# Background matmul groups of an attention and FFN kernel: where in a slot they stand and which of them share one

## The chip, the cores and the metric

The kernel runs on 1 core of a Trainium2 chip. The metric is the device time of one execution in microseconds.

## The reference

For each of 8 batches and 8 heads, `a` is the softmax of `phi` (576 x 32) over its 32 memories. From it come `k_m = a^T k` and `v_m = a^T v` (32 x 64). The scores are `q k_m^T / 8`, again with a softmax over the 32 memories, and multiplied by `v_m`. The heads are put side by side into `x` (4608 x 512), and the output is `silu(x w_in) w_out` with 2048 hidden columns. All inputs are float32.

```python
a = phi - np.max(phi, axis=2, keepdims=True)
a = np.exp(a)
a = a / (np.sum(a, axis=2, keepdims=True) + 1e-09)
k_m = np.einsum('bhsm,bhsd->bhmd', a, k)
v_m = np.einsum('bhsm,bhsd->bhmd', a, v)
```

A constant subtracted from all of `phi` in one softmax row cancels, so any shift that keeps exp in range gives the same result.

## The kernel before

**Slots.** The work goes batch by batch. A batch has 16 slots, one for each chunk `fc` of 128 hidden columns. In a slot TensorE does FFN1 of that chunk (`ffn1`, L583, twelve matmuls of 288 columns into the two banks of the tile `h`), then FFN2 of the chunk before (`main_step`, L639, with `ffn2`, L627: four tiles of 128 tokens, three matmuls of 512 columns each, into four accumulator banks). ScalarE applies silu to `h` (`silu`, L610, two activations: 512 columns into `g`, 64 leftover columns into `gleft`), and VectorE splits `g` into a high and a low float32r part (`split`, L599: a cast on L605, a subtract on L607). `h` has a single buffer, so FFN1 of the next slot waits until everything that touches `h` is done. After every second batch come four steps with the leftover tokens (`left_step`).

**Background.** While batch b runs, the attention of batch n = b + 1 is prepared by small steps, each tied to a slot (L658 to L697; `fc + 0.5` is the second half of a slot). In the order of the work they are:

- `phi_max` and `phi_fold` (VectorE): maxima of phi over the rows, folded over the partitions, so that each head and half has one value to subtract; the batch b = 0 uses `phi_allmax` with two small matmuls for it
- `phi_sub` (VectorE, L291 and L295) and `phi_exp` (ScalarE, L299)
- `e_mm`, here "e": `k_m`, `v_m` and the sums of `a`, 64 matmuls (L311) and 16 (L319) of 129 columns in array tiles of 128x32 and 64x32; its readers on VectorE and ScalarE (L327 to L335) write the normalised `kvn`
- `e_tr`, "the turn": two 128x128 transposes of `kvn` into `kvT`
- `s_mm`, the scores of one half of the tokens: 16 matmuls of 288 columns in 64x32 array tiles, then `s_turn`, two VectorE transposes back (L369)
- `s_max`, `s_sub`, `s_exp`, `s_sum`, `s_norm`, `s_back`, `s_low`: the second softmax, its transposes and the high and low part that FFN1 reads
- `p_mm`, "P": `w_in` multiplied by `v_m`, 16 matmuls of 512 columns in 64x32 array tiles for a quarter of the hidden columns (256 columns in batch 0), which ScalarE copies (L577) and VectorE subtracts (L579) into a high and a low part; FFN1 then multiplies these parts by the attention weights. A batch's own P of j = 1 to 3 stand in its slots 1, 5 and 9, and the P of j = 0 of the next batch in slot 14.

One call of a matmul on plain float32 shows as two instructions in the profile. e, the turn (from n = 2 on), the scores and P all write to one pair of banks, the tile `bg`, which also has a single buffer.

**Order.** The main loop (L803 to L823) issues FFN1, silu and split of a slot, then the first two FFN2 tiles, the steps of slot `fc`, the last two FFN2 tiles, and the steps of slot `fc + 0.5`. On TensorE and SP a written order holds up to batch 1; VectorE and ScalarE are ordered by hand only in the first stage. For the rest the framework orders the instructions of an engine by when it expects their inputs. It also puts waits between any two engines that touch one PSUM bank of a tile.

**DMA.** Loads of phi, kv, q and the stores are issued on SP. kv and q wait for the buffers that e and the scores free, phi for the one that the scores' turn back frees.

```python
            h = ffn1(b, fc)
            gs = split(silu(b, fc, h))
            for part in range(2):
                finish((2 * part, 2 * part + 1))
                for fn, a in events.pop((b, fc + part / 2), []):
                    fn(*a)
            prev = ("main", b, fc, gs)
```

Of the kernel before, what the change touches and what calls it, by code (L numbers as in the profile page):

```python
# [10 lines left out]
F32 = mybir.dt.float32  # L11
# [5 lines left out]
ALU = mybir.AluOpType  # L17
AX = mybir.AxisListType

P = 128  # L20
# [28 lines left out]
def attn_ffn_kernel(  # L49
# [149 lines left out]
    def banks(b):  # L199
# [2 lines left out]
        bg = bgtile()  # L202
        return [bg[:, 0], bg[:, 1]]

    def load_phi(b):
        t = sb.tile([P, PHW], F32, tag="att", name=f"phi{b}")
        at[b]["e"] = t[:, : FULLC * HM].rearrange("p (g c f) -> p g c f", g=2, c=FULLC)
        at[b]["er"] = t[:, FULLC * HM :]
        at[b]["et"] = t
        w = FULLC * P  # L210
        for f in ((0, w), (2 * w, PHW), (w, 2 * w)) if b == 0 else ((0, PHW),):
            load(t[:, f[0] : f[1]], phi[b, :, f[0] : f[1]])
# [17 lines left out]
    def rows(p):  # L230
        return slice(REST * p, REST * (p + 1))
# [13 lines left out]
    def phi_allmax(b, ps_=(0, 1), steps=(0, 1)):  # L245
        n = len(ps_)
        if 0 in steps:
            bank = banks(b)[0] if b else ps.tile([P, 512], F32, tag="acc", name="firstm", bufs=NI)
            pt = bank[:, : n * P]
            cm = sb.tile([P, 2], F32, tag="cm", name="cm", bufs=2)  # L250
            for i, p in enumerate(ps_):
                nc.tensor.transpose(pt[:, i * P : (i + 1) * P], at[b]["mx"][:, p], ident)
            nc.vector.tensor_reduce(cm[:, :n], pt.rearrange("p (g f) -> p g f", g=n), op=ALU.max, axis=AX.X)
            at[b]["cm"] = cm, bank[:, HM : HM + n * P]
        if 1 in steps:
            cm, pm = at[b]["cm"]
            for i in range(n):
                nc.tensor.matmul(
                    pm[:, i * P : (i + 1) * P], cm[:, i : i + 1].broadcast_to([P, P]), ident,
                    start=True, stop=True, skip_group_check=True,  # L260
                )
            at[b]["am"] = pm.rearrange("p (g f) -> p g f", g=n)

    def phi_fold(b, step):
        if step == 0:
            t = sb.tile([P, HM], F32, tag="am", name="mxt", bufs=1)
            nc.vector.transpose(t, at[b]["mx"].rearrange("p g f -> p (g f)"))
            qm = sb.tile([P, H], F32, tag="qm", name="qm", bufs=1)
            nc.vector.tensor_reduce(qm, t.rearrange("p (n m) -> p n m", m=M), op=ALU.max, axis=AX.X)
            at[b]["qm"] = qm  # L270
        elif step == 1:
            qm = at[b]["qm"]
            z = sb.tile([M, 4, H], F32, tag="qz", name="qz", bufs=1)
            for i in range(4):
                nc.vector.tensor_copy(z[:, i], qm[M * i : M * (i + 1)])  # L275
            fm = sb.tile([P, H], F32, tag="fm", name="fm", bufs=1)
            nc.vector.tensor_reduce(fm[:M], z.rearrange("p i n -> p n i"), op=ALU.max, axis=AX.X)
            for i in range(1, 4):
                nc.vector.tensor_copy(fm[M * i : M * (i + 1)], fm[:M])
            at[b]["fm"] = fm  # L280
        else:
            am = sb.tile([P, HM], F32, tag="am", name="am", bufs=1)
            wide = sb.tile([P, H, M], F32, tag="mx", name="wide", bufs=1)
            nc.vector.tensor_copy(wide, at[b]["fm"].unsqueeze(2).broadcast_to([P, H, M]))
            nc.vector.transpose(am, wide.rearrange("p n m -> p (n m)"))
            at[b]["am"] = am.rearrange("p (g f) -> p g f", g=2)

    def phi_sub(b, ps_=(0, 1)):
        e, er, am = at[b]["e"], at[b]["er"], at[b]["am"]
        g = slice(ps_[0], ps_[-1] + 1)  # L290
        nc.vector.tensor_tensor(  # L291
            e[:, g], e[:, g], am.unsqueeze(2).broadcast_to([P, len(ps_), FULLC, P]), op=ALU.subtract
        )
        for i, p in enumerate(ps_):
            nc.vector.tensor_tensor(er[rows(p)], er[rows(p)], am[rows(p), i], op=ALU.subtract)  # L295

    def phi_exp(b, ps_=(0, 1)):
        if len(ps_) == 2:
# [5 lines left out]

    def e_mm(b):
        e, er, kvt, kr = (at[b][k] for k in ("e", "er", "kv", "kr"))
        pt = banks(b)
        turns = [(c, p) for c in range(FULLC) for p in range(2)]
        for c, p in turns:
            for r in range(NR):  # L310
# [24 lines left out]
                nc.vector.tensor_scalar(kvn[:, :, p], src, rs[p], None, op0=ALU.mult)  # L335

    def e_tr(b):
        if b > 1:
            bg = bgtile()
            pt = [bg[:, 0, P * kind : P * (kind + 1)] for kind in range(2)]  # L340
        else:
            pt = [live["h"][:, kind, HALF : HALF + P] for kind in range(2)]
        t = sb.tile([P, 2, NR, M], F32, tag="kvT", name=f"kvT{b}", bufs=2)
        for kind in range(2):
            nc.tensor.transpose(pt[kind], kvn[:, kind].rearrange("p g d -> p (g d)"), ident)
        nc.vector.tensor_copy(t[:, 0].rearrange("p r m -> p (r m)"), pt[0])
        nc.scalar.copy(t[:, 1].rearrange("p r m -> p (r m)"), pt[1])
        at[b]["kvT"] = t

    def s_mm(b, hf):  # L350
        if "sc" not in at[b]:
# [304 lines left out]
        events.setdefault((b, slot), []).append((fn, a))  # L656

    for b in range(B):  # L658
        if b == 0:
            for j in range(2, DFF // CW):  # L660
                ev(b, 2 * j - 1.5, p_mm, b, j * CW, CW)
        else:
            for j in range(1, NJ):
                ev(b, 4 * j - 3, p_mm, b, j * JW, JW)
        n = b + 1
        if n == B:
            continue
        at_slot = (4, 5, 6, 7.5, 9, 9.5, 11.5, 11.5, 12, 12.5, 12.5, 13) if b == 0 else (0, 1, 2, 3, 4, 6, 7, 8, 9, 10, 11, 12)
        mx, sub, ex, em, tr, s0, s1, sx, se, ss, sn, sk = at_slot
        ev(b, mx, phi_max, n)  # L670
        if n == 1:
# [8 lines left out]
        if n + 1 < B:  # L680
            ev(b, 14 if b == 0 else em + 1, load_kv, n + 1)
        ev(b, tr, e_tr, n)
        ev(b, s0, s_mm, n, 0)
        ev(b, em, load_q, n, 1)
        ev(b, s1, s_mm, n, 1)
        if n + 1 < B:
            ev(b, s1, load_q, n + 1, 0)
        ev(b, sx, s_max, n, ALL)
# [15 lines left out]
        getattr(mybir.EngineType, e) for e in ("PE", "DVE", "Activation", "SP")  # L704
    )
    whole = ExitStack()
    whole.enter_context(in_order(PE, SP))
    load_phi(0)
    I0, O0, I1 = ("i", 0), ("o", 0), next(to_conv)
    idle = ps.tile([P, 2, 512], F32, tag="h", name="idle", bufs=1)[:, 0]  # L710
# [92 lines left out]
    for b in range(B):  # L803
        if b == 1:
            whole.close()
        for fc in range(NFC):
            if b == 0 and fc < 2:
# [3 lines that stand above are left out]
                continue  # L811
            h = ffn1(b, fc)
            gs = split(silu(b, fc, h))
            for part in range(2):
                finish((2 * part, 2 * part + 1))
                for fn, a in events.pop((b, fc + part / 2), []):
                    fn(*a)
            prev = ("main", b, fc, gs)
        if b % 2:
            for n in range(NLS):  # L820
                gs = split(gleft[:, n * NI : (n + 1) * NI].rearrange("p c f -> p (c f)"))
                finish((0, 1, 2, 3))
                prev = ("left", b, n, gs)  # L823
# [56 lines left out]
```

## Time and profile before

| | us |
|---|---|
| median of 3 runs (lowest to highest) | 713.63 (712.69 to 713.66) |
| the profiled execution, its own time | 711.86 |
| its span, first to last instruction | 710.1 |
| TensorE matmuls busy | 696.2 (98%) |
| VectorE busy | 366.3 (52%) |
| ScalarE busy | 258.5 (36%) |

The granted TensorE clock is 0.999 of full speed over the span. The chain of work that ended last lies to 83% on TensorE. The profile names TensorE's matmuls PE, its weight loads PEld, VectorE DVE, ScalarE ACT and SyncE SP. A line of the timeline gives the start and the duration in us, then engine, line, operation, the tiles written and read, the array tile, shape and count; the bracket at its end is the engine's idle time before it and what released it. Matmuls are pipelined: their durations overlap, so what a matmul costs is read from the distance between starts.

### The profile page before, as it was taken

Reading aid. Unit: us, or ns where it says so; the run is one execution under the profiler, and the core shown is the slowest. Engines: PE = TensorE matmul, PEld = TensorE weight load, DVE = VectorE, ACT = ScalarE, POOL = GpSimd, SP = SyncE. Lnnn points to the kernel's source line nnn. Section 1 sums busy time; section 2 is a strip of 40 time slices with the busy share of each in tenths; the row PEclk is TensorE's granted clock in tenths of the full one; section 3 lists DMA queues with packets and bytes.
Section 4 is the critical chain, followed back from the end, with each engine's and each line's share of the span. In section 5 each row is a group of like instructions: output and inputs, shape, how many; then the busy total and the mean of one; then the engine's idle time right before and its main releaser. Section 6 shows DMA issues by size and latency. Waiting matters only on the chain.

```text
span 710.1 us, 11571 instructions
## 1 busy us (share of the span) xinstructions
PE 696.2 (98%) x4833; PEld 556.1 (78%) x4833; DVE 366.3 (52%) x658; ACT 258.5 (36%) x454; POOL 0.7 (0%) x6
## 2 busy tenths in 40 slices
PE   7899999999999999999999999999999999999997
PEld 3577678788888788777887778887888878888885
DVE  3899886355353563538246373535635356233322
ACT  2789854233323332424224241423322323222211
POOL 0000000000000000000000000000000000000000
PEclk9999999999999999999999999999999999999999
DMA  9977615321113210232011420132101000010002
GB/s 341 387 243 235 245 38 224 135 67 35 45 31 135 67 34 1 83 146 68 1 60 20 153 76 3 61 135 67 34 15 60 2 1 1 0 61 1 1 1 74
DMA packets 25444, 60.14 MB, mean 85 GB/s; under 512 B 2096, under 2 KB 10416, under 8 KB 25392
## 3 DMA queue, kind: packets, MB, share of 16 engines
q1 hardware_dynamic: 24672, 57.02, 23.0%
q10 hardware_dynamic: 720, 2.38, 0.9%
q8 instruction: 38, 0.62, 0.4%
q14 instruction: 14, 0.11, 0.1%
HBM read 49.95 MB, written 9.44 MB: 84 GB/s over the span
## 4 chain that ended last, share of the span: by engine, by line
PE 83%; DVE 3%; ACT 2%; DMA 1%; issue 0%; ACTq 0%
PE acc L627 44%; PE h L593 25%; PE accleft L627 6%; PE bg L563 4%; PE bg L311 2%; PE bg L357 1%; DMA raw<-in_w_out 1%; DVE gparts L607 1%; ACT L613 1%; DVE phi L291 1%; ACT phi L299 0%; ACT pparts L577 0%; PE bg L319 0%; DVE qz L275 0%; ACT g L613 0%
## 5 line engine op out<-in xcount | busy, mean ns | idle before, releaser
L627 PE MATMUL acc<-wo_hi,gparts 128*128 128x512 f32 x1024 | 352.5, 397 | 0.3 <-DVE gparts L607 0.3
L627 PEld LDWEIGHTS acc<-wo_hi,gparts 128*128 128x128 f32 x1024 | 191.9, 188 | 66.9 <-issue 29.8
L593 PEld LDWEIGHTS h<-aparts,pparts 128*128 128x128 f32 x1536 | 215.2, 188 | 17.8 <-ACT gleft L615 4.7
L593 PE MATMUL h<-aparts,pparts 128*128 128x288 f32 x1536 | 225.9, 296 | 1.6 <-ACT gleft L615 0.8
L627 PE MATMUL acc<-wo_lo,gparts 128*128 128x512 f32 x512 | 201.2, 393 | 0.4 <-DVE wo_lo L176 0.4
L613 ACT ACTIVATE g<-h 128x512 f32<-128x512 f32 x128 | 76.4, 597 | 303.4 <-issue 175.4
L605 DVE CAST gparts<-g 128x512 fp32r<-128x512 f32 x128 | 54.5, 426 | 222.0 <-ACT g L613 221.2
L627 PEld LDWEIGHTS acc<-wo_lo,gparts 128*128 128x128 f32 x512 | 96.1, 188 | 15.2 <-DVE wo_lo L176 0.7
L607 DVE TENSOR_TENSOR gparts<-g,gparts 128x512 fp32r<-128x512 f32 x128 | 88.2, 689 | 10.5 <-DVE gparts L605 0.5
L579 DVE TENSOR_TENSOR pparts<-bg,pparts 128x1024 fp32r<-128x1024 f32 (+1 forms) x36 | 39.6, 1099 | 36.2 <-ACT pparts L577 36.2
L577 ACT ACTIVATE pparts<-bg 128x1024 fp32r<-128x1024 f32 (+1 forms) x36 | 33.4, 927 | 27.8 <-PE bg L563 27.8
L627 PE MATMUL accleft<-wo_hi,gparts 128*128 128x512 f32 x128 | 40.6, 389 | 0.0
L563 PE MATMUL bg<-win,kvT 64*32 64x512 f32 (+1 forms) x576 | 35.8, 554 | 0.9 <-DVE kvn L335 0.9
L615 ACT ACTIVATE gleft<-h 128x64 f32<-128x64 f32 x128 | 28.0, 218 | 0.0
L627 PEld LDWEIGHTS accleft<-wo_hi,gparts 128*128 128x128 f32 x128 | 24.0, 188 | 4.9
L633 ACT ACTIVATE o<-acc 128x512 f32<-128x512 f32 x32 | 19.2, 599 | 21.9 <-PE acc L627 10.7
L627 PE MATMUL accleft<-wo_lo,gparts 128*128 128x512 f32 x64 | 24.9, 389 | 0.0
L613 ACT ACT_TABLE_LOAD x14 | 18.0, 1283 | 8.0 <-PE h L593 7.9
L563 PEld LDWEIGHTS bg<-win,kvT 64*32 64x32 f32 x576 | 6.5, 104 | 14.1 <-issue 11.7
L605 DVE CAST gparts<-gleft 128x512 fp32r<-128x512 f32 x16 | 6.8, 427 | 20.3 <-PE accleft L627 11.9
L168 ACT ACTIVATE raw<-raw 128x1024 int32<-128x1024 uint32 (+1 forms) x16 | 16.7, 1041 | 0.0
L395 DVE TENSOR_REDUCE ssm<-sc 128x36 f32<-128x1152 f32 x7 | 9.5, 1354 | 8.8 <-ACT sc L391 8.8
(126 smaller groups left out, 365.6 us busy)
## 6 DMA issues: line engine op xcount, KB each, us to landing
kv<-in_kv SPq DMA_DIRECT2D x28, 516.0 KB, 5.7
q<-in_q SPq DMA_DIRECT2D x16, 576.0 KB, 3.8
out<-o SPq DMA_DIRECT2D x32, 256.0 KB, 2.1
raw<-in_w_in SPq DMA_DIRECT2D x14, 512.0 KB, 6.4
raw<-in_w_out SPq DMA_DIRECT2D x6, 1024.0 KB, 7.3
phi<-in_phi SPq DMA_DIRECT2D x7, 576.0 KB, 3.7
kv<-in_kv ACTq DMA_DIRECT2D x4, 516.0 KB, 6.0
kr<-in_kv SPq DMA_DIRECT2D x7, 258.0 KB, 7.2
```

The source lines that it names most:

```text
L168: nc.scalar.activation(r, low, AF.Copy, scale=2.0**-29)
L311: nc.tensor.matmul(pt[p][M * r : M * (r + 1), :KVW], e[:, p, c, M * r : M * (r + 1)], kvt[c][:, p, r], start=c == 0, stop=False, skip_grou ...
L563: nc.tensor.matmul(bg[M * r : M * (r + 1), p, :w].rearrange("p (k f) -> p k f", f=P), kvT[D * p : D * (p + 1), 1, r], win[D * p : D * (p + ...
L577: nc.scalar.activation(hi[:, :, c], bg[:, :, :w], AF.Copy)
L579: nc.vector.tensor_tensor(lo[:, :, c], bg[:, :, :w], hi[:, :, c], op=ALU.subtract)
L593: nc.tensor.matmul(h[:, hf, :HALF], wt[:, p, fs], a[:, p, sl], start=n == 0, stop=n == 5)
L605: nc.vector.tensor_copy(ghi, g32)
L607: nc.vector.tensor_tensor(glo, g32, ghi, op=ALU.subtract)
L613: nc.scalar.activation(g32.rearrange("p (h f) -> p h f", h=2), h[:, :, :w], AF.Silu)
L615: nc.scalar.activation(gleft[:, fc, o : o + LEFT].rearrange("p (h f) -> p h f", h=2), h[:, :, w:HALF], AF.Silu)
L627: nc.tensor.matmul(acc[key], gt[:, cs], wt[:, fc], start=fc == 0 and n == 0, stop=fc == NFC - 1 and n == 2)
L633: nc.scalar.activation(o, acc.pop(key), AF.Copy)
```

## The change

From batch 1 on all steps of a slot, those of `fc` and of `fc + 0.5`, are issued behind FFN1 and ahead of all twelve FFN2 matmuls; batch 0 keeps its halves. For n from 2 to 7 the slots are new:

| step | before | after |
|---|---|---|
| phi_max, phi_fold with phi_sub, phi_exp | 0, 1, 2 | 1, 2, 3 |
| e | 3 | 5 (behind P of j = 2) |
| the turn | 4 | 9 (behind P of j = 3) |
| scores | 6 and 7 | 10, both halves in one group |
| s_max and s_sub, s_exp | 8, 9 | 11, 12 |
| s_sum, s_norm | 10, 11 | 13 |
| s_back, s_low, load of the next phi | 12 | 14 |
| loads: q second half, next kv, next q first half | 3, 4, 7 | 5, 6, 10 |

e and the turn no longer write to `bg` but to the columns of h's two banks behind the 288 that FFN1 uses (`beside_h`). The scores of both halves (`s_all`) put 512 of the 576 columns into `bg` and the last 64 beside h, as three runs of 16 instructions (288, 224 and 64 columns). Their transposes become two of 512 columns and two of 64. `phi_sub` subtracts each half of phi by an instruction of its own, with that half's maxima; for batch 0 this also means that the first half, which so far took the second half's maxima, takes its own. TensorE's order is now written for the whole kernel.

```diff
@@ -202,6 +202,10 @@
         bg = bgtile()
         return [bg[:, 0], bg[:, 1]]
 
+    def beside_h(w):
+
+        return [live["h"][:, i, HALF : HALF + w] for i in range(2)]
+
     def load_phi(b):
         t = sb.tile([P, PHW], F32, tag="att", name=f"phi{b}")
         at[b]["e"] = t[:, : FULLC * HM].rearrange("p (g c f) -> p g c f", g=2, c=FULLC)
@@ -259,7 +263,8 @@
                     pm[:, i * P : (i + 1) * P], cm[:, i : i + 1].broadcast_to([P, P]), ident,
                     start=True, stop=True, skip_group_check=True,
                 )
-            at[b]["am"] = pm.rearrange("p (g f) -> p g f", g=n)
+            for i, p in enumerate(ps_):
+                at[b]["am", p] = pm[:, i * P : (i + 1) * P]
 
     def phi_fold(b, step):
         if step == 0:
@@ -283,16 +288,17 @@
             wide = sb.tile([P, H, M], F32, tag="mx", name="wide", bufs=1)
             nc.vector.tensor_copy(wide, at[b]["fm"].unsqueeze(2).broadcast_to([P, H, M]))
             nc.vector.transpose(am, wide.rearrange("p n m -> p (n m)"))
-            at[b]["am"] = am.rearrange("p (g f) -> p g f", g=2)
+            for p in range(2):
+                at[b]["am", p] = am[:, p * P : (p + 1) * P]
 
     def phi_sub(b, ps_=(0, 1)):
-        e, er, am = at[b]["e"], at[b]["er"], at[b]["am"]
-        g = slice(ps_[0], ps_[-1] + 1)
-        nc.vector.tensor_tensor(
-            e[:, g], e[:, g], am.unsqueeze(2).broadcast_to([P, len(ps_), FULLC, P]), op=ALU.subtract
-        )
-        for i, p in enumerate(ps_):
-            nc.vector.tensor_tensor(er[rows(p)], er[rows(p)], am[rows(p), i], op=ALU.subtract)
+        e, er = at[b]["e"], at[b]["er"]
+        for p in ps_:
+            am = at[b]["am", p]
+            nc.vector.tensor_tensor(
+                e[:, p], e[:, p], am.unsqueeze(1).broadcast_to([P, FULLC, P]), op=ALU.subtract
+            )
+            nc.vector.tensor_tensor(er[rows(p)], er[rows(p)], am[rows(p)], op=ALU.subtract)
 
     def phi_exp(b, ps_=(0, 1)):
         if len(ps_) == 2:
@@ -304,7 +310,7 @@
 
     def e_mm(b):
         e, er, kvt, kr = (at[b][k] for k in ("e", "er", "kv", "kr"))
-        pt = banks(b)
+        pt = banks(b) if b < 2 else beside_h(KVW)
         turns = [(c, p) for c in range(FULLC) for p in range(2)]
         for c, p in turns:
             for r in range(NR):
@@ -335,17 +341,34 @@
                 nc.vector.tensor_scalar(kvn[:, :, p], src, rs[p], None, op0=ALU.mult)
 
     def e_tr(b):
-        if b > 1:
-            bg = bgtile()
-            pt = [bg[:, 0, P * kind : P * (kind + 1)] for kind in range(2)]
-        else:
-            pt = [live["h"][:, kind, HALF : HALF + P] for kind in range(2)]
+        pt = beside_h(P)
         t = sb.tile([P, 2, NR, M], F32, tag="kvT", name=f"kvT{b}", bufs=2)
         for kind in range(2):
             nc.tensor.transpose(pt[kind], kvn[:, kind].rearrange("p g d -> p (g d)"), ident)
         nc.vector.tensor_copy(t[:, 0].rearrange("p r m -> p (r m)"), pt[0])
         nc.scalar.copy(t[:, 1].rearrange("p r m -> p (r m)"), pt[1])
         at[b]["kvT"] = t
+
+    def s_all(b):
+
+        sc = at[b]["sc"] = sb.tile([P, 2, S], F32, tag="att", name=f"sc{b}")
+        bg, left = bgtile(), beside_h(S - 512)
+        kvT = at[b]["kvT"]
+        w = 512 - HALF
+        for hf, f, n in ((0, 0, HALF), (1, 0, w), (1, w, HALF - w)):
+            for r in range(NR):
+                for p in range(2):
+                    to = left[p] if f else bg[:, p, hf * HALF : hf * HALF + n]
+                    nc.tensor.matmul(
+                        to[M * r : M * (r + 1)],
+                        kvT[D * p : D * (p + 1), 0, r],
+                        at[b]["q", hf][D * p : D * (p + 1), r, f : f + n],
+                        start=True, stop=True, skip_group_check=True,
+                    )
+        for p in range(2):
+            nc.vector.transpose(sc[:, p, :512], bg[:, p])
+        for p in range(2):
+            nc.vector.transpose(sc[:, p, 512:], left[p])
 
     def s_mm(b, hf):
         if "sc" not in at[b]:
@@ -656,16 +679,16 @@
         events.setdefault((b, slot), []).append((fn, a))
 
     for b in range(B):
+        n = b + 1
         if b == 0:
             for j in range(2, DFF // CW):
                 ev(b, 2 * j - 1.5, p_mm, b, j * CW, CW)
         else:
             for j in range(1, NJ):
                 ev(b, 4 * j - 3, p_mm, b, j * JW, JW)
-        n = b + 1
         if n == B:
             continue
-        at_slot = (4, 5, 6, 7.5, 9, 9.5, 11.5, 11.5, 12, 12.5, 12.5, 13) if b == 0 else (0, 1, 2, 3, 4, 6, 7, 8, 9, 10, 11, 12)
+        at_slot = (4, 5, 6, 7.5, 9, 9.5, 11.5, 11.5, 12, 12.5, 12.5, 13) if b == 0 else (1, 2, 3, 5, 9, 10, 10, 11, 12, 13, 13, 14)
         mx, sub, ex, em, tr, s0, s1, sx, se, ss, sn, sk = at_slot
         ev(b, mx, phi_max, n)
         if n == 1:
@@ -680,9 +703,12 @@
         if n + 1 < B:
             ev(b, 14 if b == 0 else em + 1, load_kv, n + 1)
         ev(b, tr, e_tr, n)
-        ev(b, s0, s_mm, n, 0)
         ev(b, em, load_q, n, 1)
-        ev(b, s1, s_mm, n, 1)
+        if n == 1:
+            ev(b, s0, s_mm, n, 0)
+            ev(b, s1, s_mm, n, 1)
+        else:
+            ev(b, s0, s_all, n)
         if n + 1 < B:
             ev(b, s1, load_q, n + 1, 0)
         ev(b, sx, s_max, n, ALL)
@@ -704,7 +730,8 @@
         getattr(mybir.EngineType, e) for e in ("PE", "DVE", "Activation", "SP")
     )
     whole = ExitStack()
-    whole.enter_context(in_order(PE, SP))
+    ctx.enter_context(in_order(PE))
+    whole.enter_context(in_order(SP))
     load_phi(0)
     I0, O0, I1 = ("i", 0), ("o", 0), next(to_conv)
     idle = ps.tile([P, 2, 512], F32, tag="h", name="idle", bufs=1)[:, 0]
@@ -812,9 +839,12 @@
             h = ffn1(b, fc)
             gs = split(silu(b, fc, h))
             for part in range(2):
-                finish((2 * part, 2 * part + 1))
+                if b == 0:
+                    finish((2 * part, 2 * part + 1))
                 for fn, a in events.pop((b, fc + part / 2), []):
                     fn(*a)
+            if b:
+                finish(range(NI))
             prev = ("main", b, fc, gs)
         if b % 2:
             for n in range(NLS):
```

## Rows read from the trace of the kernel before

**Rows 1.** The page's costliest groups: FFN1's matmuls (busy, mean ns; idle before, releaser)

```profile
L593 PE MATMUL h<-aparts,pparts 128*128 128x288 f32 x1536 | 225.9, 296 | 1.6 <-ACT gleft L615 0.8
```

**Rows 2.** Timeline, PE, one slot without background work (start us, duration us)

```profile
172.26 1.75 PE L593 MATMUL h<-aparts,pparts 128*128 128x288 f32 x12
...
176.58 1.75 PE L593 MATMUL h<-aparts,pparts 128*128 128x288 f32 x12
```

**Rows 3.** Timeline, PE, around one P of 512 columns, batch 1 slot 9

```profile
160.53 0.40 PE L627 MATMUL acc<-wo_lo,gparts 128*128 128x512 f32 x1
160.76 0.40 PE L627 MATMUL acc<-wo_hi,gparts 128*128 128x512 f32 x1
161.09 1.09 PE L563 MATMUL bg<-win,kvT 64*32 64x512 f32 x16
162.11 0.50 PE L627 MATMUL acc<-wo_hi,gparts 128*128 128x512 f32 x1
162.45 0.40 PE L627 MATMUL acc<-wo_lo,gparts 128*128 128x512 f32 x1
```

**Rows 4.** Timeline, PE, one P of 256 columns at a slot's end, batch 0

```profile
61.91 0.66 PE L563 MATMUL bg<-win,kvT 64*32 64x256 f32 x16
62.51 1.72 PE L593 MATMUL h<-aparts,pparts 128*128 128x288 f32 x11
```

**Rows 5.** Timeline, PE, around e, batch 1 slot 3

```profile
129.06 0.39 PE L627 MATMUL acc<-wo_hi,gparts 128*128 128x512 f32 x1
129.37 1.97 PE L311 MATMUL bg<-kv,phi 128*32 128x129 f32 x64
131.27 0.45 PE L319 MATMUL bg<-kr,phi 64*32 64x129 f32 x16
...
131.99 0.39 PE L627 MATMUL acc<-wo_lo,gparts 128*128 128x512 f32 x1
```

**Rows 6.** Timeline, PE, FFN2 matmuls around one score group, batch 1 slot 7

```profile
151.24 0.40 PE L627 MATMUL acc<-wo_hi,gparts 128*128 128x512 f32 x1
...
152.55 0.40 PE L627 MATMUL acc<-wo_lo,gparts 128*128 128x512 f32 x1
```

**Rows 7.** Timeline, PE and ACT, batch 1 slot 2 to slot 3: exp and silu

```profile
121.64 1.75 PE L593 MATMUL h<-aparts,pparts 128*128 128x288 f32 x12
...
122.05 1.17 ACT L299 ACTIVATE phi<-phi 128x1152 f32<-128x1152 f32 x1 [1.71 <-DVE phi L295]
...
124.15 1.28 ACT L613 ACT_TABLE_LOAD   x1
...
125.94 0.22 ACT L615 ACTIVATE gleft<-h 128x64 f32<-128x64 f32 x1
...
126.21 1.85 PE L593 MATMUL h<-aparts,pparts 128*128 128x288 f32 x12
```

**Rows 8.** Timeline, DVE, batch 1 slots 1 and 2: maxima, subtraction, P's split

```profile
116.09 0.45 DVE L267 STREAM_TRANSPOSE mxt<-mx 128x256 f32<-128x256 f32 x1
...
121.73 0.29 DVE L295 TENSOR_TENSOR phi<-phi,am 64x128 f32<-64x128 f32 x1
124.16 1.23 DVE L579 TENSOR_TENSOR pparts<-bg,pparts 128x1024 fp32r<-128x1024 f32 x1 [2.15 <-ACT pparts L577]
```

**Rows 9.** Timeline, ACT and DVE, the slot of rows 2: silu's and the split's ends

```profile
174.58 0.22 ACT L615 ACTIVATE gleft<-h 128x64 f32<-128x64 f32 x1
...
175.25 0.69 DVE L607 TENSOR_TENSOR gparts<-g,gparts 128x512 fp32r<-128x512 f32 x1
```

**Rows 10.** Timeline, DVE, the last reader of e and one pair of score transposes

```profile
132.68 0.35 DVE L335 TENSOR_SCALAR kvn<-bg,rs 128x128 f32<-128x128 f32 x1 [0.43 <-ACT kvn L333]
...
152.39 0.85 DVE L369 STREAM_TRANSPOSE sc<-bg 128x288 f32<-128x288 f32 x2 [0.20 <-PE bg L357]
```

**Rows 11.** The page's DMA issues: phi (count, KB each, us to landing)

```profile
phi<-in_phi SPq DMA_DIRECT2D x7, 576.0 KB, 3.7
```

**Rows 12.** Timeline, ACT, start of the kernel: a wait for weights

```profile
17.87 0.66 ACT L166 ACTIVATE win<-raw 128x512 f32<-128x512 f32 x1 [1.08 <-DMA raw<-in_w_in]
```

## The prediction

> **What bounds the kernel now.** I read the page's group of the FFN1 matmuls first. Over the whole run TensorE stood idle 1.6 us before them [rows 1]: the end is set by what TensorE is given to do, and other engines matter only where they make it wait. Next I read TensorE's timeline slot by slot, from the first FFN1 matmul of one slot to that of the next. A slot without background work takes 176.58 - 172.26 = 4.32 us, call it 4.33 [rows 2]. Whatever a slot takes beyond that is background or a wait, so each edit can be priced as a difference to 4.33.
>
> P costs a slot this much: the FFN2 matmuls around it start 162.45 - 160.76 = 1.69 us apart where two spacings of 0.23 would be 0.46, so 1.23 us [rows 3]. It has parts. Entry: P's first matmul starts 0.33 after the last FFN2 one, not 0.23, so 0.10. Exit: the first FFN2 matmul after P takes 0.34 to the next, so 0.11. In between 1.02, while the half as wide P of batch 0 takes 62.51 - 61.91 = 0.60 [rows 4]; so 256 columns cost 0.42, and 0.18 is there whatever the width. The fixed price of any 64x32 group in this kernel is then 0.10 + 0.11 + 0.18 = 0.39 us, plus 0.42 per 256 columns.
>
> By the same reading e costs 131.99 - 129.06 - 0.46 = 2.47 us [rows 5], and one of the two score groups 152.55 - 151.24 - 0.46 = 0.85 us [rows 6]; the formula gives 0.39 + 0.47 = 0.86 for its 288 columns.
>
> One slot a batch waits. FFN1 of slot 3 should start 4.33 after 121.64, at 125.97, and starts at 126.21: 0.24 us late, and its row is 1.85 us instead of 1.75, so 0.34 in all [rows 2, 7]. It waits for silu's last read of h, which ended at 126.16. ScalarE had first idled 1.71 us for the maxima's subtraction, ran exp (1.17), P's copy, a table load (1.28), and only then silu.
>
> **The change, part by part.** The new slots hold in batches 1 to 6, where batches 2 to 7 are prepared: six times each.
>
> Moving P (and the scores) from between FFN2's halves to behind FFN1. P is 3 x 7 + 6 = 27 groups there, the scores 6. Exit and inside stay. The entry now drains a 288-column matmul instead of a 512-column one, which no row shows. It could be free (-0.10), or still take 0.33 where FFN1 to FFN2 takes less, about 0.10 more. Over 33 groups that is -3.3 to +3.3 us. I take 0: the 0.10 is an addition to the spacing of the matmul before it, and only that spacing changes. FFN2 itself is only shifted inside its slot; the operands it reads were made a slot earlier.
>
> P and e in one slot. One exit and one entry fall away: 0.21 us. Bounds: 0, if the switch from 64*32 to 128*32 costs as much as both, to 0.39, the whole fixed price [rows 3]. P and the turn: the transposes are full-array like FFN2, they only change neighbours; 0, at best the exit of 0.11.
>
> The two score groups as one. Now 1.70 us. Then one fixed price, 0.39, and 288 + 224 = 512 columns into bg, 0.84, and 16 more matmuls of 64 columns beside h. By columns these cost 0.10. By the instruction rate of e, 64 in 131.27 - 129.37 = 1.90 us or 0.030 each, they cost 0.48 [rows 5]. e keeps four sub-arrays busy and the scores eight, so I take half of that rate, 0.24, between the two. Sum 1.47, a saving of 0.23; bounds -0.01 to 0.37.
>
> The Trainium skill, in TensorEngine Tiling (Array Packing), section Instruction Overhead, speaks against this cut: a matmul there carries about 60 cycles however few columns it has. An estimate by it, with sixteen such matmuls one behind the other at 2.4 GHz, is 0.40 us for the pieces, and the saving would be 0.07 instead of 0.23. No row here has a matmul that narrow.
>
> exp a slot later. Today the fold starts at 116.09, as its slot 1 starts, and the last subtraction ends at 122.02, 5.93 later [rows 8]. A slot later on the same terms it ends 5.93 - 4.33 = 1.6 after slot 3 starts. It could be earlier by 1.9, since slot 1 is 5.56 long with P and VectorE has finished that slot's cast and subtract at 3.68 [rows 9]; or later by 1.23, if P's split, which P's earlier place brings forward, gets in front [rows 8]. So -0.3 to 2.8. From there exp, table load and silu take 1.17 + 1.28 + 0.73 = 3.18 [rows 7], and FFN1 starts 0.05 behind silu, so it needs them by 4.28. At 1.6 that is 0.5 late plus the restart of 0.10, at -0.3 nothing, at 2.8 it is 1.8; if exp stands behind silu of slot 3 it is nothing either. The middle of the orders that keep silu of slot 2 in front is near the point where the wait begins, because P's copy is no longer queued between exp and the table load; I take 0.10. Gain 0.34 - 0.10 = 0.24; bounds 0.34 and -1.5.
>
> Splitting the subtraction by halves adds one VectorE start per batch. VectorE is idle much of each slot, so I price it at nothing beyond the chain above. At the start of the kernel the first half no longer needs the second half's maxima, but soon after ScalarE waits 1.08 us for weights from DMA [rows 12], so being earlier buys nothing: 0, at best 1.1.
>
> DMA issues on SP's queue. q's second half, kv, q's first half and phi are asked for two or three slots later. Each still waits only for buffers that its own batch frees, and is read a batch later; the shortest is phi, asked for behind the turn back of the scores around slots 13 and 14 and read in slot 1 or later. That leaves two slots, 8.7 us, for a load of 3.7 [rows 2, 11]. Behind it on SP stand only the stores of slot 15. Price 0; if phi came later than that, VectorE's chain of the paragraph above would start later by as much.
>
> The sum: 0.21 + 0.23 + 0.24 = 0.68 us per batch, six times 4.1 us. The profiled execution took 711.86 us with a span of 710.1; it would take 707.8. The median of the three runs is 713.63, 1.77 above the profiled one; from there the forecast is 709.5 us, 0.6% less. About 0.2%, 1.4 us, is what a measurement of this kernel can tell from no change.
>
> **The rivals.** First, exp queued too early. The new kernel leaves ScalarE's order to the scheduler, and today exp runs ahead of P's copy, which belongs to an earlier slot [rows 7, 8]. If exp comes before silu of slot 2, silu waits for a chain that ends 5.93 after slot 2's start, or 1.9 less, and ends 3.18 after that: FFN1 of slot 3 is 2.9 to 4.8 us late. Six times 3.9 is 23.4 us, against it stand the other gains, 6 x 0.44 = 2.6, and today's wait, 6 x 0.34 = 2.0: 713.6 - 4.6 + 23.4, about 732 us. It decides as soon as the new wait exceeds 0.78 a batch. For it: VectorE's chain is as long as a slot. Against it: silu of a slot is done 2.54 after the slot starts [rows 9], before the subtraction can be. 6%.
>
> Second, h held too long, the rival on the slower side that I rate highest. e, the turn and the last score columns now live in h's banks, and the next FFN1 needs h. In front: silu has read h at 174.80 - 172.26 = 2.54 [rows 9], and FFN1 has 4.33 - 12 x 0.23 = 1.57 us, so P runs from about 1.7 to 2.7 and e begins just behind silu. At the end: e's sums need 133.03 - 131.72 = 1.3 us [rows 5, 10] and FFN2's 12 x 0.23 give 2.8, a margin of 1.5. The scores have the least: cast and subtract until 3.68, then transposes of the same columns as two pairs of 0.85 [rows 9, 10], until 5.4, and FFN1 is due at 4.33 + 1.47 = 5.8. If one VectorE operation of 1.23 gets in front, FFN1 is 0.8 late, with the restart 0.9: six times 5.6 us, 715.1. It decides from a wait of 0.68 a batch. 10%.
> The Trainium skill, in PSUM — Partial Sum Buffer, section Summary: rules for kernel authors, asks that what is read while a matmul runs lie in another bank, and this change does the opposite. By that rule each group beside h has to stand behind silu's reads; the rows leave 0.1 us of room for that in front.
>
> Third, the gains are smaller: the narrow pieces at e's full rate and 0.4 of waiting at slot 3 leave 0.21 - 0.01 - 0.06 = 0.14 a batch, 0.8 us: 712.8. 10%.
>
> **How the numbers follow.** The forecast and its neighbours, all faster by over 0.2%, have 74%; the third rival, no difference, 10%; the two slower ones 16%. The likeliest case gives 709.5. Its best terms together (0.39 + 0.37 + 0.34 a batch) would be 6.6 us, 707.0, which is the low end; the range reaches up through the third rival and most of the way to the second, 714.6, and leaves out some 2 in 10: the first rival, the second one's worse half, and entries that turn out cheaper or dearer than taken.
>
> **What would show it.** Slot 5 near 4.33 + 1.23 + 2.26 = 7.8 us, slot 10 near 5.8, slot 9 near 5.6 to 5.8, slots with P alone still 5.56, and slot 3 to slot 4 within 0.1 of 4.33. FFN1's idle time before it should fall from 1.6. I am wrong if FFN1 of slots 3, 4, 6 or 11 waits for silu or for a VectorE read of h, or if P behind FFN1 costs anything but 1.23.

## The result, and the profile after

The median of ten runs after is 715.54 us (714.43 to 716.73), against 713.01 us (711.97 to 715.95) of ten runs of the kernel before on the same chip: a ratio of 1.0035, with an interval of 1.0024 to 1.0047. The change made the kernel slower by a third of a per cent; the forecast was 709.5 us, and the range to 714.6 did not hold it. The profiled execution of after took 714.7 us with a span of 712.9, at a granted TensorE clock of 1.000 (0.999 before), so the clock does not explain it. Executions of one kernel differ by up to 4 us, in part with the granted clock (the six of run 2 below: 709.67 and 709.73 us at 0.993 and 0.994, the others 705.76 to 707.65 at 0.996 to 1.000), so the slots of the profiled executions are compared beside the medians.

The first view is the page of the kernel after: its span, the engines of the chain that ended last, and two of its groups of instructions (busy, mean ns of one | idle time before, what ended it).

```profile
span 712.9 us, 11772 instructions
...
PE 78%; DVE 6%; ACT 4%; issue 3%; DMA 2%; SPq 0%; ACTq 0%; DVEq 0%
...
L616 PE MATMUL h<-aparts,pparts 128*128 128x288 f32 x1536 | 225.7, 296 | 7.2 <-ACT gleft L638 6.9
...
L414 ACT ACTIVATE sc<-sc 128x1152 f32<-128x1152 f32 x7 | 8.2, 1167 | 25.2 <-DVE sc L410 25.2
```

FFN1 is now L616. TensorE idled 1.6 us before it in the kernel before [rows 1] and 7.2 now, and 6.9 of that ends with silu's second half, `gleft`. In the chain TensorE's share fell from 83% to 78%, while DVE rose from 3% to 6% and ACT from 2% to 4%. The last row is the exp of the second softmax: ScalarE stood idle 25.2 us in front of it, always for VectorE's subtraction; in the kernel before that wait was 0.3 us in all. The list of waits shows how these waits fall, as total us, times, longest:

```profile
ACT sc L414 <- DVE sc L410: 25.2, 7, 4.1
...
PE h L616 <- ACT gleft L638: 6.9, 7, 1.0
...
PEld h L317 <- ACT gleft L638: 5.0, 6, 0.8
...
PEld acc L650 <- DVE gparts L630: 3.4, 9, 0.6
```

Seven waits of up to 1.0 us, where the kernel before had one of 0.8 us in all [rows 1]: six are new, one in each of batches 1 to 6. The slots of batch 2, read from TensorE's timeline as in the prediction (from FFN1 to FFN1), place it. The last column is the kernel of the first experiment below.

| slots of batch 2, us | before | after | exp behind silu |
|---|---|---|---|
| 1 and 14 (P alone), each | 5.57 | 5.54 | 5.54 |
| 2, 3, 4 together | 16.04 | 12.99 | 12.99 |
| 5 | 5.57 | 7.84 | 7.84 |
| 6 and 7 together | 10.40 | 8.66 | 8.66 |
| 9 | 5.57 | 5.72 | 5.72 |
| 10 | 4.33 | 5.73 | 5.73 |
| 11 | 4.33 | **5.50** | 4.33 |
| 12 | 4.33 | **4.65** | 4.33 |
| the whole batch | 79.02 | 79.47 | 77.96 |

Batches 3 to 6 repeat this within 0.05 us a slot, apart from slot 15, where every second batch does its leftover tokens. Slots 11 and 12 have no background work on TensorE in either kernel. They take 1.17 and 0.32 us longer than a clean slot [rows 2], over the six batches 1.48 on average and 8.9 us in all. TensorE's timeline of after, batch 2, slots 5 and 10:

```profile
225.52 1.74 PE L616 MATMUL h<-aparts,pparts 128*128 128x288 f32 x12
227.19 1.09 PE L586 MATMUL bg<-win,kvT 64*32 64x512 f32 x16
228.21 1.97 PE L317 MATMUL h<-kv,phi 128*32 128x129 f32 x64
230.11 0.45 PE L325 MATMUL h<-kr,phi 64*32 64x129 f32 x16
230.49 0.50 PE L650 MATMUL acc<-wo_hi,gparts 128*128 128x512 f32 x1
...
252.06 1.74 PE L616 MATMUL h<-aparts,pparts 128*128 128x288 f32 x12
253.73 1.09 PE L362 MATMUL bg<-q,kvT 64*32 64x288 f32 x32
254.66 0.35 PE L362 MATMUL h<-q,kvT 64*32 64x64 f32 x16
254.94 0.50 PE L650 MATMUL acc<-wo_hi,gparts 128*128 128x512 f32 x1
```

e follows P without a gap, 1.02 us after P's start, and the scores run as one group. What the change does on TensorE is there as the diff says. The timeline of all engines in slots 10 to 12 of the same batch, with only the rows that bear on it, shows the new wait:

```profile
253.90 0.60 ACT L636 ACTIVATE g<-h 128x512 f32<-128x512 f32 x1 [3.38 <-PE h L616]
254.63 1.28 ACT L414 ACT_TABLE_LOAD   x1
255.67 1.30 DVE L369 STREAM_TRANSPOSE sc<-bg 128x512 f32<-128x512 f32 x2
256.90 0.34 DVE L371 STREAM_TRANSPOSE sc<-h 128x64 f32<-128x64 f32 x2
257.27 1.35 DVE L406 TENSOR_REDUCE smx<-sc 128x36 f32<-128x1152 f32 x1
257.79 1.75 PE L616 MATMUL h<-aparts,pparts 128*128 128x288 f32 x12
258.65 1.36 DVE L410 TENSOR_TENSOR sc<-sc,smx 128x1152 f32<-128x1152 f32 x1
260.05 1.17 ACT L414 ACTIVATE sc<-sc 128x1152 f32<-128x1152 f32 x1 [4.14 <-DVE sc L410]
261.23 1.28 ACT L636 ACT_TABLE_LOAD   x1
262.52 0.60 ACT L636 ACTIVATE g<-h 128x512 f32<-128x512 f32 x1
263.02 0.22 ACT L638 ACTIVATE gleft<-h 128x64 f32<-128x64 f32 x1
263.29 1.87 PE L616 MATMUL h<-aparts,pparts 128*128 128x288 f32 x12 [1.01 <-ACT gleft L638]
263.50 1.35 DVE L424 TENSOR_TENSOR sc<-sc,ssm 128x1152 f32<-128x1152 f32 x1
264.76 0.68 DVE L630 TENSOR_TENSOR gparts<-g,gparts 128x512 fp32r<-128x512 f32 x1
265.50 0.74 PE L650 MATMUL acc<-wo_hi,gparts 128*128 128x512 f32 x2
```

Slot 11 starts at 257.79, and its `h` is complete about 1.7 us later. ScalarE does not read it: exp of the second softmax is next in its queue, its table already loaded at 254.63, and it waits for VectorE until 260.05. Only behind exp and another table load does silu run, 262.52 to 263.24. FFN1 of slot 12 was due at 257.79 + 4.33 = 262.12 and starts at 263.29. Its row is then 1.87 us instead of 1.75, the restart that the prediction put at 0.10; and the late silu sends the cast of `g` late into VectorE, where the softmax's multiplication by the reciprocal sums (263.50) gets in front of the second part of the split (264.76 to 265.44), and FFN2 waits for that at 265.50. The two make up the 0.32 us of slot 12. In the kernel before ScalarE did this in the other order. Its timeline in batch 1, slots 8 and 9:

```profile
155.53 0.60 ACT L613 ACTIVATE g<-h 128x512 f32<-128x512 f32 x1 [4.49 <-issue]
156.03 0.22 ACT L615 ACTIVATE gleft<-h 128x64 f32<-128x64 f32 x1
156.26 1.28 ACT L391 ACT_TABLE_LOAD   x1
157.56 1.17 ACT L391 ACTIVATE sc<-sc 128x1152 f32<-128x1152 f32 x1
```

There silu of slot 8 came first and exp behind it.

### The profile page after: what moved, and what is told of

Same layout as the page of the kernel before. It is cut to its first block, busy times and chain, and to the rows that moved or that the text cites. A ratio compares the mean times of both kernels' runs of the same rounds, so it can differ in the third digit from the quotient of the medians.

```text
span 712.9 us, 11772 instructions
## 1 busy us (share of the span) xinstructions
PE 693.5 (97%) x4929; PEld 562.3 (79%) x4929; DVE 364.6 (51%) x665; ACT 260.1 (36%) x454; POOL 0.7 (0%) x6
## 4 chain that ended last, share of the span: by engine, by line
PE 78%; DVE 6%; ACT 4%; issue 3%; DMA 2%; SPq 0%; ACTq 0%; DVEq 0%
PE acc L650 41%; PE h L616 24%; PE accleft L650 6%; PE bg L586 4%; PE h L317 2%; ACT g L636 1%; DMA raw<-in_w_in 1%; ACT L636 1%; DVE sc L410 1%; DVE smx L406 1%; DVE sc L369 1%; DVE gparts L628 1%; ACT raw L168 0%; DMA out<-o 0%; PE h L347 0%
## 5 line engine op out<-in xcount | busy, mean ns | idle before, releaser
L650 PE MATMUL acc<-wo_hi,gparts 128*128 128x512 f32 x1024 | 342.9, 396 | 0.2 <-DVE gparts L630 0.2
L616 PEld LDWEIGHTS h<-aparts,pparts 128*128 128x128 f32 x1536 | 215.2, 188 | 23.3 <-ACT gleft L638 10.4
L616 PE MATMUL h<-aparts,pparts 128*128 128x288 f32 x1536 | 225.7, 296 | 7.2 <-ACT gleft L638 6.9
L414 ACT ACTIVATE sc<-sc 128x1152 f32<-128x1152 f32 x7 | 8.2, 1167 | 25.2 <-DVE sc L410 25.2
L317 PEld LDWEIGHTS h<-kv,phi 128*32 128x32 f32 x384 | 10.2, 110 | 5.0 <-ACT gleft L638 5.0
```

The lines of the kernel that those rows point to most:

```text
L317: nc.tensor.matmul(pt[p][M * r : M * (r + 1), :KVW], e[:, p, c, M * r : M * (r + 1)], kvt[c][:, p, r], start=c == 0, stop=False, skip_grou ...
L616: nc.tensor.matmul(h[:, hf, :HALF], wt[:, p, fs], a[:, p, sl], start=n == 0, stop=n == 5)
L650: nc.tensor.matmul(acc[key], gt[:, cs], wt[:, fc], start=fc == 0 and n == 0, stop=fc == NFC - 1 and n == 2)
```

## The experiments

My theory was that this order alone, exp ahead of silu in ScalarE's queue, costs more than the rest of the change gains. Rivals were that the new place of the background groups costs something, that sharing h's banks does, and that TensorE's written order, which keeps other work out of a wait, decides. Runs 1 to 4 were on one chip beside 20 runs of the kernel before (median 712.68 us), and runs 5 to 8 on another beside 19 (712.64). "Exp behind silu" below means an order without a semaphore between two instructions of ScalarE (`behind`, a helper of one line that the diffs below do not show). The diffs hold the changed lines, with the part of them that changes; `...` stands between places.

**1. exp of the second softmax behind silu.** The kernel after, with exp tied behind silu of slot 11 and its step in that slot.

```diff
-        nc.scalar.activation(v, v, AF.Exp, scale=SCALE)
+        i = nc.scalar.activation(v, v, AF.Exp, scale=SCALE); b > 1 and behind(i, live["silu"])
...
-        nc.scalar.activation(
+        live["silu"] = nc.scalar.activation(
...
-(1, 2, 3, 5, 9, 10, 10, 11, 12, 13, 13, 14)
+(1, 2, 3, 5, 9, 10, 10, 11, 11, 13, 13, 14)
```

> The changed kernel with one edit: the second softmax's exp is tied behind silu of slot 11 in ScalarE's queue (batches 1 to 6). Theory A, exp ahead of silu of slot 11 makes FFN1 of slot 12 wait: in the changed kernel slots 11 and 12 take 5.50 and 4.64 us where 4.33 each is normal, 1.48 a batch; they should go back to 4.33, six times 1.48 = 8.9 us less, span 712.9 -> 704.0, time 715.5 -> 706.6. Theory B, h is held too long by the scores beside it: the score's reads are not touched, slot 11 keeps a wait of about 1.2 us and the time stays at 715. Theory C, the place of P and the scores behind FFN1 costs by itself: nothing changes, 715.

It took 708.09 us, a ratio to before of 0.9933 (0.9917 to 0.995); the profiled execution took the 706.6 expected (706.59), the other five 706.93 to 709.66. Its page shows FFN1's idle time as

```profile
L616 PE MATMUL h<-aparts,pparts 128*128 128x288 f32 x1536 | 225.0, 295 | 1.2 <-ACT gleft L638 0.8
```

and ScalarE's timeline in batch 2, slot 11, the order of before:

```profile
258.92 0.60 ACT L636 ACTIVATE g<-h 128x512 f32<-128x512 f32 x1 [5.02 <-PE h L616]
259.41 0.22 ACT L638 ACTIVATE gleft<-h 128x64 f32<-128x64 f32 x1
259.65 1.28 ACT L414 ACT_TABLE_LOAD   x1
260.94 1.17 ACT L414 ACTIVATE sc<-sc 128x1152 f32<-128x1152 f32 x1
```

Slots 11 and 12 are clean in all six batches (table above); all other slots stay as in after. From the first FFN1 of batch 1 to that of batch 7 this kernel takes 501.10 us, after 509.98: the difference of 8.88 is six times 1.48. This version beats both kernels.

**2. The same order for phi's exp too.** Run 1 with one more tie. In batch 1 of after, slots 3 and 4 take 4.91 and 4.43 us, a wait that the other batches don't have; there phi's exp is ahead of silu of slot 3.

```diff
-            nc.scalar.activation(at[b]["et"], at[b]["et"], AF.Exp)
+            i = nc.scalar.activation(at[b]["et"], at[b]["et"], AF.Exp); b > 1 and behind(i, live["silu"])
```

> As the first run, and the exp of phi is also tied behind silu of its slot 3. In the changed kernel only batch 1 waits there (slots 3 and 4 take 4.91 and 4.43 us, 0.68 over normal). Theory A for that wait too: 0.68 us less than the first run, 705.9, if exp a slot's part later delays nothing (e is two slots on). Theory B and C: no difference to the first run, or slower if silu of slot 4, which now needs the table load, comes later than 4.28 us after its slot's start.

707.51 us, 0.9929 (0.9909 to 0.995): no measurable step from run 1. Slot 4 of batch 1 is clean, but slot 3 still takes 4.81; 0.2 of the 0.68 came back, half in each. The rest has another cause, which the timeline of batch 1 shows on VectorE and TensorE:

```profile
128.50 0.41 DVE L628 CAST gparts<-g 128x512 fp32r<-128x512 f32 x1
128.94 0.29 DVE L301 TENSOR_TENSOR phi<-phi,am 64x128 f32<-64x128 f32 x1
129.26 0.69 DVE L630 TENSOR_TENSOR gparts<-g,gparts 128x512 fp32r<-128x512 f32 x1
...
130.01 0.73 PE L650 MATMUL acc<-wo_hi,gparts 128*128 128x512 f32 x2 [0.21 <-DVE gparts L630]
```

Slot 2's split stands behind the chain of phi's maxima and subtractions on VectorE and ends at 129.95, and FFN2 of slot 3 waits for it. That is an order on VectorE, not on ScalarE, and most of this run's expectation fell. In after the same wait of FFN2 stands in slot 3 of batch 1, and silu's overlaps it for the most part.

**3. The place undone.** The kernel after with the steps between the FFN2 halves again.

```diff
-                if b == 0:
+                if True:
                     finish((2 * part, 2 * part + 1))
...
-            if b:
+            if False:
                 finish(range(NI))
```

> The changed kernel with only the placement undone: the steps of a slot stand again between the halves of FFN2 (and, for half slots, behind them); which slots they have, e and the turn beside h, the scores in one group all stay. The scores then come 1.4 us later in slot 10, and exp falls behind silu of slot 11 in ScalarE's queue without being tied. Theory A: no wait before FFN1 of slot 12; what is new is that e's and the scores' readers have 1.4 us instead of 2.8 before the next FFN1, so small waits of 0 to 0.5 at slots 6 and 11; 706.6 plus 0 to 6, about 709. Theory B: h is held even longer, slower than the changed kernel, 718. Theory C: P between the halves is cheaper or dearer than behind FFN1 by the difference to the first run; A says 1.23 to 1.24 a P as before.

710.48 us, 0.9966 (0.9954 to 0.9978). exp falls behind silu of slot 11 by itself, with nothing tied, as ScalarE's timeline of batch 2 shows:

```profile
259.33 0.22 ACT L638 ACTIVATE gleft<-h 128x64 f32<-128x64 f32 x1
...
260.86 1.17 ACT L414 ACTIVATE sc<-sc 128x1152 f32<-128x1152 f32 x1
```

The wait at slot 12 is gone: the place in the program was enough to turn ScalarE's order. But slots 1, 5, 9 and 14 are each 0.02 to 0.03 longer than in run 1, slot 6 is 0.05, slot 10 0.26 and slot 11 0.06 longer, 0.48 a batch in all. With the groups later in the slot, the readers of e and of the scores' last columns end later, and FFN1 of slots 6 and 11 comes late for h (slot 11 is taken up below). So the new place by itself is a gain, 2.4 us by the medians of runs 1 and 3; batch 1, which is free of its wait at slot 3 here, gives 0.7 of it back.

**4. The kernel before with exp ahead.** The kernel before, with s_max and s_sub half a slot earlier, exp in the same step, and silu of slot 8 tied behind it.

```diff
-(0, 1, 2, 3, 4, 6, 7, 8, 9, 10, 11, 12)
+(0, 1, 2, 3, 4, 6, 7, 7.5, 7.5, 10, 11, 12)
...
-        nc.scalar.activation(v, v, AF.Exp, scale=SCALE)
+        i = nc.scalar.activation(v, v, AF.Exp, scale=SCALE); b > 1 and live.update(exp=i)
...
-        nc.scalar.activation(g32.rearrange("p (h f) -> p h f", h=2), h[:, :, :w], AF.Silu)
+        i = nc.scalar.activation(g32.rearrange("p (h f) -> p h f", h=2), h[:, :, :w], AF.Silu); "exp" in live and behind(i, live.pop("exp"))
```

> The kernel before with one edit: the second softmax's exp stands ahead of silu of slot 8 in ScalarE's queue, not behind it; nothing else. Theory A: the subtraction ended at 156.02, 2.32 us after that slot's start; exp, table load and silu take 3.18, so FFN1 of slot 9 starts at 5.55 instead of 4.33, 1.2 late and 0.1 of restart; six times 1.3 = 7.9 us, 713.0 -> 720.9. Theories B and C: the kernel before has neither groups beside h in these batches nor P behind FFN1, so nothing should change but exp's own place: 713.

714.03 us, 1.0011 (1.0001 to 1.0021): a miss by 7 us. TensorE's timeline in batch 2, at the end of slot 8, says why:

```profile
249.47 0.39 PE L627 MATMUL acc<-wo_hi,gparts 128*128 128x512 f32 x1
249.79 1.09 PE L563 MATMUL bg<-win,kvT 64*32 64x512 f32 x16
250.96 1.85 PE L593 MATMUL h<-aparts,pparts 128*128 128x288 f32 x12
```

FFN1 is 1.26 us late as expected (slot 8 takes 5.59 instead of 4.33), but the whole P of slot 9 has moved into the wait, and slot 9 falls from 5.57 to 4.43. In the kernel before TensorE's order is written only until batch 1 begins.

**5. The same with TensorE's order written to the end.** One edit more than run 4:

```diff
-    whole = ExitStack()
-    whole.enter_context(in_order(PE, SP))
+    whole = ExitStack(); ctx.enter_context(in_order(PE))
+    whole.enter_context(in_order(SP))
```

> The earlier run with exp ahead of silu in the kernel before cost only 1 us: its profile shows that P of slot 9 had moved to the end of slot 8, into the wait. So the same edit again, and TensorE's order written for the whole kernel as the change does, so that nothing can move. Theory A: FFN1 of slot 9 starts 5.55 after slot 8 instead of 4.33, and 0.1 of restart: 1.3 a batch, 7.9 us, 713 -> 720.6. If A is wrong and exp's place does not matter in itself: 714 as without the fixed order.

721.68 us, 1.0124 (1.0109 to 1.0139). The list of waits has the line of after again, at another line of the code:

```profile
PE h L593 <- ACT gleft L615: 7.4, 7, 1.1
```

Slots 8 and 9 take 5.59 and 5.86: 1.55 us a batch more than before, 9.3 in six, and 9.04 by the medians. The order on ScalarE, put into the kernel before without any other part of the change but the written order, makes the wait of after in kind and in size. The written order alone was not run there; but all other slots of this run are within 0.01 us of before, so it costs nothing that shows.

**6. The kernel after with TensorE's order free from batch 1 on**, as before.

```diff
-    ctx.enter_context(in_order(PE))
-    whole.enter_context(in_order(SP))
+    whole.enter_context(in_order(PE, SP))
```

> The changed kernel with TensorE's order written up to batch 1 only, as in the kernel before. Five of the eight matmul calls of P of slot 14 then stand ahead of FFN1 of slot 12, in the wait. Theory A with filling: the wait of 1.17 us a batch is used, but a part of P takes nearly as long as all of it, since the eight sub-arrays work side by side, and the other three calls still cost about 1.2 us in slot 14; so the gain is small, 0 to 0.3 a batch, 713.5 to 715.5. Rival: the fixed order is what made the change slow, P's part fills the wait and is gone from slot 14 in proportion: 5/8 of 1.23, 0.77 a batch, 4.6 us, 711.

714.34 us, 1.0023 (1.0013 to 1.0032). The framework now moves part of the P of slot 14 into the wait, as TensorE's timeline in batch 2 shows:

```profile
263.75 1.07 PE L586 MATMUL bg<-win,kvT 64*32 64x512 f32 x10
264.84 1.86 PE L616 MATMUL h<-aparts,pparts 128*128 128x288 f32 x12
...
275.26 1.06 PE L586 MATMUL bg<-win,kvT 64*32 64x512 f32 x6
```

But the six instructions that are left take as long as sixteen, and slot 14 falls only from 5.54 to 5.51. Slot 12 takes 4.43 instead of 4.65: the restart is left, and FFN2's wait for VectorE is not there, why is not shown. Together this gives back some 0.25 of the 1.48 us. The written order costs the kernel after little: what the framework found for the wait was a part of one group.

**7. e without P in front.** Run 1 with e, and the loads that go with it, a slot later, alone beside h.

```diff
-(1, 2, 3, 5, 9, 10, 10, 11, 11, 13, 13, 14)
+(1, 2, 3, 6, 9, 10, 10, 11, 11, 13, 13, 14)
```

> The first run (exp behind silu of slot 11) with e moved from slot 5, behind P, to slot 6, alone behind FFN1. Theory: P does two things for e, it shares the entry and exit (0.21 us) and it covers silu's read of h's banks. Without P e would start 1.69 us after the slot's start, and silu has read h at 2.54: a wait of 0.85 and more, so slots 5 and 6 together take 5.54 + 4.33 + 2.47 + 0.85 = 13.2 instead of 7.84 + 4.33 = 12.17, six times 1.0 to 1.1 us: 708.1 -> 714.4. Rival: e and silu touch different columns of the banks and do not wait for each other: only 0.2 a batch, 709.4.

713.61 us, 1.0015 (1.0003 to 1.0028). Slots 5 and 6 take 5.54 + 7.76 = 13.30 instead of 12.17, 1.13 a batch. Rows of ScalarE's and TensorE's timelines in slot 6 of batch 2:

```profile
231.89 1.74 PE L616 MATMUL h<-aparts,pparts 128*128 128x288 f32 x12
...
234.20 0.22 ACT L638 ACTIVATE gleft<-h 128x64 f32<-128x64 f32 x1
...
234.47 1.75 PE L317 MATMUL h<-kv,phi 128*32 128x129 f32 x56 [0.85 <-ACT gleft L638]
```

Beside h, e has to wait for silu's reads of the same banks, 0.85 us, unless P stands in front of it.

**8. The scores in two groups.** Run 2 with the two halves in slots 10 and 11, both into `bg`; their exp is tied behind silu of slot 12.

```diff
-(1, 2, 3, 5, 9, 10, 10, 11, 11, 13, 13, 14)
+(1, 2, 3, 5, 9, 10, 11, 11, 12, 13, 13, 14)
...
-        if n == 1:
+        if n >= 1:
             ev(b, s0, s_mm, n, 0)
             ev(b, s1, s_mm, n, 1)
```

> The second run (both exps behind silu) with the scores as two groups of 288 columns in bg in slots 10 and 11, each behind FFN1, instead of one group with 64 columns beside h; exp then is tied behind silu of slot 12. By the changed kernel's slot 10, 5.73 or 1.40 over normal, and 0.85 to 0.87 for a group of its own: slots 10 and 11 take 10.36 to 10.40 instead of 10.06, 0.3 to 0.34 a batch, 2 us: 707.5 -> 709.5. If the narrow matmuls cost more than thought the difference is smaller; if chain steps one slot later make anything wait, larger.

707.78 us, 0.9929 (0.9914 to 0.9944). Slots 10 and 11 take 5.17 each, 10.34 instead of 5.73 + 4.33 = 10.06, which is 1.7 us in six batches. Against run 2 the medians differ by 0.3 us, less than these runs can tell. By the slots one group is worth 0.28 a batch; the measured times lean that way where the granted clock is alike (at 0.996 or more run 2's four executions took 705.76 to 707.65, run 8's four 707.46 to 708.30), but do not settle it.

## Why the prediction was wrong

**The step that failed** is the one that was left out of the sum. The change moves the scores, s_max, s_sub and s_exp from slots 6 to 9 to slots 10 to 12, and the prediction priced the scores by TensorE's columns and the rest of that row at nothing, without naming the work that hides it. It asked where exp would stand against silu for phi's exp alone, its first rival, and put that at 6%. The same question holds for the second exp, and there it decided: exp ahead of silu, FFN1 of the next slot 1.17 late, 0.3 more in that slot for the restart and the wait for VectorE, 8.9 us in six batches. Runs 1 and 5 show this from both sides, taking it away and putting it in. Nor did the list of slots whose FFN1 must not wait (3, 4, 6, 11) hold slot 12.

**The second rival's** 715.1 us came close to 715.54, but not by its mechanism. It had VectorE's transposes hold h against FFN1 of slot 11. That FFN1 came on time in after, since slot 10 takes 5.73 us and has no wait. That the time came out so close is chance. Only in run 3, with the groups later in the slot, does such a wait appear: VectorE's transposes from h end at 256.77 in batch 2, FFN1 of slot 11 starts at 256.91 instead of 256.65, 0.26 late:

```profile
256.43 0.34 DVE L371 STREAM_TRANSPOSE sc<-h 128x64 f32<-128x64 f32 x2
...
256.91 1.82 PE L616 MATMUL h<-aparts,pparts 128*128 128x288 f32 x12
```

**The terms that were priced** came in, and more. In run 1, where the new wait is away, they can be read alone, from batch 2:

| term, us per batch | forecast | measured | from |
|---|---|---|---|
| P alone behind FFN1, slots 1 and 14 | 0 | 0.06 | twice 5.57 to 5.54 |
| P and e in one slot | 0.21 | 0.20 | 1.24 + 2.47 to 7.84 - 4.33 = 3.51 |
| P and the turn | 0 | 0.09 | 1.24 + 0.24 to 5.72 - 4.33 = 1.39 |
| scores as one group | 0.23 | 0.34 | twice 0.87 to 5.73 - 4.33 = 1.40 |
| exp of phi | 0.24 | 0.34 | 16.04 less e and the turn to 12.99 |
| sum | 0.68 | 1.03 | |

By their whole length batches 2 to 6 gain 1.06 to 1.13 us each, and batch 1, which keeps a wait of 0.7 in slots 3 and 4, 0.41: from the first FFN1 of batch 1 to that of batch 7 it is 506.94 - 501.10 = 5.84. The medians of run 1 show 712.68 - 708.09 = 4.6 where 4.1 were forecast; the profiled execution of run 1 reached batch 1 0.69 us later than that of before.

**The entry of P** was right to be near nothing: P starts 1.67 after FFN1 where FFN2 starts 1.58 after it, so the addition is still 0.09, and the exit is 0.11 as before [rows 3].

**The narrow pieces** beside h cost less than the 0.24 taken. Slot 10 exceeds a slot with P alone, also one group of 512 columns, by 5.73 - 5.54 = 0.19 us: that is what 16 matmuls of 64 columns add, together with cutting the 512 columns into 288 and 224, at most 0.012 for each of the sixteen. In the trace their starts lie within 0.13 us, in two rounds of eight. The Trainium skill, TensorEngine Tiling (Array Packing), section Instruction Overhead, has about 60 cycles for every matmul however narrow; by that the prediction's estimate for the sixteen, one behind the other, was 0.40. The trace has half of it: the overhead does not add up along these sixteen, which go to eight sub-arrays.

**Sharing h's banks** was free in after only because of what stands in front. In the list of waits above, e's weight loads (PEld, L317) wait 5.0 us in six batches for silu's last read of h, while P runs. Run 7 shows the price without P, 0.85 us of waiting and 1.13 us a batch in all. The Trainium skill, PSUM — Partial Sum Buffer, section Summary: rules for kernel authors, asks for another bank where a matmul runs beside a read; run 7 shows a price of not doing so, the framework's wait, and no run here shows a collision in the bank. Slot 5 of after shows that a group into another bank covers the wait.

**exp of phi** was priced at a subtraction that ends 1.6 us after slot 3 starts and a wait from there. In batch 1 it ended 127.49 - 125.85 = 1.64 after, and silu held FFN1 of slot 4 to 130.76, 0.58 late, as priced. But by then FFN2 of slot 3 had already waited for VectorE's split, and run 2, which took silu's lateness away, got back 0.2 of the 0.68: the rest is VectorE's order, which the prediction priced at nothing beyond the chain of phi. In batch 2 the subtraction ended 0.8 after (217.68 against 216.87), and there silu ended at 220.91, in time for FFN1 at 221.20. The forecast of that chain fitted one batch in six, and the others did better.

**What else was priced at nothing** stayed so: the profiled execution of after reached batch 1 at 111.66 us, that of before at 111.74, and no slot of batches 2 to 6 waited for a load of phi, kv or q.

**What stays open** is why the framework's scheduler put the second exp ahead of silu of slot 11. Run 3 shows that the place of the steps ahead of FFN2 turns the order, not by which of its estimates.

## What to carry to other kernels

When a chain across engines is moved to other slots, list for each in-order queue that it passes what it will stand in front of: an instruction that waits for a long chain also holds back everything queued behind it, and on ScalarE here a table load of 1.28 us stands between exp and the silu behind it. Price this for every moved chain, not for the one that waits today; when the scheduler picks the order, either forecast both orders or write the order down. A wait for a shared bank can be covered by a group that goes to another bank, and the cover is then part of the design.

## What was not expected of the hardware

Six of P's sixteen instructions, alone, took a row of 1.06 us, ten 1.07, and all sixteen 1.09 (run 6 and the timeline of after). Splitting such a group costs almost its whole time again. The single starts in the traces show how: sixteen stand in two rounds of eight, 0.01 us apart inside a round, the second round 0.45 after the first; ten stand in two rounds of five and six in two rounds of three, and the second round again starts 0.45 and 0.46 after the first. Three, five or eight of these matmuls side by side take the same time here. The whole P of slot 9, moved into a wait in run 4, gave back 1.14 of the 1.26 us that the wait cost.
